# Four small groups of products per batch, issued as two pairs

## The chip, the cores and the metric

The kernel runs on one core of a Trainium2 chip. A core has a matrix engine (TensorE, PE in the profile; its weight loads are shown as PEld), a vector engine (VectorE, DVE), an activation engine (ScalarE, ACT), a general engine (GpSimd, POOL) and a queue engine that issues transfers (SyncE, SP). The metric is the time of one execution on the device, in microseconds (us); the median of several runs counts.

## The reference

The kernel computes a Fourier mixing followed by a feed-forward block with the quick form of GELU. The input x has 8 batches of 3008 rows and 256 columns.

```
X = fft(x, axis=1); X = fft(X, axis=2); y = X.real      # (8, 3008, 256) -> (24064, 256)
h = y @ w_in                                            # 256 -> 2048
g = h * (1 / (1 + exp(-1.702 * h)))
out = g @ w_out                                         # 2048 -> 256
```

## The kernel before

The transform along the 3008 rows is split, 3008 = 47 × 64. A first stage makes transforms of length 47 and a second stage transforms of length 64. The transform along the 256 columns is folded into the weights w_in before the main loop starts.

The main loop has 384 steps: 8 batches, 3 blocks to a batch, 2 halves to a block, and 8 pairs of feed-forward columns (p) to a half. So one batch lasts 48 steps. The order of work is written by hand: every engine has its own queue and works it off in the order in which the program issues to it. A step t issues, in this order:

- `hidden(t)` (L478): eight products with the folded weights, of 256 or 225 columns, into two banks, `pa` and `pb`, and on ScalarE a copy `v` of `pa` (L482). A product in float32 stands as two records in the profile, so `pa` and `pb` have four each.
- `product(t - 3)` (L551): seven products of the second layer (14 records), into banks of their own, `po`.
- `activate(t - 1)` on ScalarE (L507), then `sums(t - 1)` on GpSimd (L519, L520) and `sums(t - 2)` on VectorE (L522, L523).
- `rows(t)` on VectorE: L492 reads `v` and `pb`, L495 (twice) reads `pb`, L502 reads `pa`. After L495 the bank of `pb` is free, after L502 that of `pa`.
- every eighth step `combine` on VectorE (L585, L568), and output transfers from SP (L610).
- the extras of this step, from a table that is filled by `at(step, function, ...)`. They prepare the next batch.

The extras of a batch that starts at step t0 are (three steps later in the first batch): eight folds `fold1` on GpSimd (L195 to L202), one every second step from t0 + 7 on, that add and subtract rows of the next batch's tile `xt` in place; four groups of first-stage products `mix1` (L226) at t0 + 10, 14, 18 and 22, each one step after the second of the two folds that it needs; then `spill` of the result to memory at t0 + 24 (L302), `fill` from there in another layout at t0 + 29 (L308), the load of a further batch at t0 + 33 (L178). The second stage `stage2` (L328) comes at t0 + 8, 16 and 24.

One `mix1` group has eight products of 47 rows by 64 columns of weights (16 records). They go to the four quarters of the array in turn, since each needs only a quarter of it. The first group of a batch has 11 products (22 records), as one of its products is replaced by four of 127 to 129 columns from a small tile `e`. A group writes two banks, `ps[0]` and `ps[1]`, and then ScalarE copies each of them back into `xt` (L229).

`pa`, `pb`, the two banks of `mix1`, those of `stage2` and some small ones all come from one pool of four banks:

```
psm = ctx.enter_context(tc.tile_pool(name="psm", bufs=4, space=PS))
def bank(name):
    return psm.tile([128, 512], F32, tag="mm", name=name)
```

A tile takes a bank as soon as its earlier user has been read for the last time. In the program before, the products of `hidden` that follow a group take the banks of the `hidden` just ahead of the group: `pa` waits for L495 of that step, `pb` for L502. The step after that takes the banks of the group, behind its copies L229.

Of the kernel before, what the change touches and what calls it, by code (L numbers as in the profile page):

```python
# [111 lines left out]
def kernel(ctx: ExitStack, tc, x, w_in, w_out, tab1, tab2, out):  # L112
# [605 lines left out]
    def at(t, fn, *args):  # L718
        extra.setdefault(t, []).append((fn, args))
# [19 lines left out]
    for b in range(B):  # L739
        t0 = b * NBLK * NF  # L740
        late = 0 if b else 3
        if b + 2 < B:
            at(t0 + 10, turn, b + 2)
        if b + 1 < B:
            for c in range(NCH):
                at(t0 + 7 + 2 * c + late, fold1, b + 1, c, nc.gpsimd)
                if c % 2:
                    at(t0 + 8 + 2 * c + late, mix1, b + 1, c // 2)
            at(t0 + 24 + late, spill, b + 1)
            at(t0 + 29 + late, fill, b + 1)  # L750
            if b + 2 < B:
                at(t0 + 33 + late, load_x, b + 2)
            at(t0 + 36 + late, rotate, b + 1)
        for blk in range(NBLK):
            nxt = (b, blk + 1) if blk + 1 < NBLK else (b + 1, 0)
            if nxt[0] < B:
                at(t0 + blk * NF + 8, stage2, *nxt)
                at(t0 + blk * NF + 12, nyquist, *nxt)
# [53 lines left out]
```

## Time and profile before

| | |
|---|---|
| median of 6 runs | 1921.02 us (1920.35 to 1922.67) |
| the profiled execution's own time | 1922.67 us |
| its span, from the first to the last instruction | 1920.9 us |
| granted TensorE clock, mean over the span | 0.999 |
| TensorE busy | 1906.7 us, 99% |
| VectorE, ScalarE, GpSimd busy | 1419.4 us (74%), 674.7 us (35%), 761.4 us (40%) |
| L226, first-stage products | 490 records in 28 groups |
| L229, copies of their results | 56, 0.589 us each in the median |

The profile's chain follows the work back from the last instruction, always to what released it, and gives the share of each engine and line in that chain. The timeline gives rows of merged instructions: start in us, length in us, engine, line, operation, output<-inputs, sizes and count; a bracket behind a row says how long the engine was idle ahead of it and what ended that. The ends of products are modelled, so their starts are the better measure.

### The profile page before, as it was taken

The numbers are of one execution on the slowest core, as the hardware profiler recorded it, in microseconds if no ns is written. First come the engines' busy times: TensorE is split into PE (matmuls) and PEld (weight loads), VectorE is DVE, ScalarE is ACT, GpSimd is POOL, SyncE is SP. The second block draws the span as 40 slices with busy tenths as digits, with TensorE's granted clock in tenths as the row PEclk, the third lists the DMA queues.
The fourth block names the chain that finished last, engine by engine and source line by source line (L and its number), as shares of the span: only waits on it lengthen the run. The fifth ranks groups of instructions, "written<-read, shape, count | busy, mean of one in ns | idle before, by whom it ended". The sixth has DMA issues, their size and how long they took to land.

```text
span 1920.9 us, 29354 instructions
## 1 busy us (share of the span) xinstructions
PE 1906.7 (99%) x10720; PEld 1673.4 (87%) x10720; DVE 1419.4 (74%) x2937; ACT 674.7 (35%) x932; POOL 761.4 (40%) x1057
## 2 busy tenths in 40 slices
PE   8999999999999999999999999999999999999998
PEld 5798888988889888988889888898888988889887
DVE  7777677877787677777777777677777777778766
ACT  6533333333333333333333333333333333333332
POOL 4475224633246223552235523264323642223222
PEclk9999999999999999999999999999999999999999
DMA  8721530335212542226222272121820223202201
GB/s 267 177 50 34 114 37 12 59 53 106 17 22 49 91 67 23 52 27 103 44 28 50 43 105 34 16 49 43 124 19 12 17 49 56 17 12 27 17 12 23
DMA packets 145312, 103.54 MB, mean 54 GB/s; under 512 B 104914, under 2 KB 127986, under 8 KB 143984
## 3 DMA queue, kind: packets, MB, share of 16 engines
q1 hardware_dynamic: 143952, 101.14, 31.4%
q8 instruction: 85, 1.39, 0.3%
q10 hardware_dynamic: 1216, 0.52, 0.1%
q14 instruction: 59, 0.48, 0.1%
HBM read 58.38 MB, written 48.01 MB: 55 GB/s over the span
## 4 chain that ended last, share of the span: by engine, by line
PE 98%; DMA 1%; DVE 1%; POOL 0%; issue 0%; SPq 0%; ACT 0%; ACTq 0%; POOLq 0%
PE po L551 59%; PE pa L478 18%; PE pb L478 17%; PE ps L226 2%; PE ps L328 1%; DMA raw<-in_moe_w_in_dram 1%; PE psw L444 1%; DMA wo<-in_tab_dram 0%; POOL wst L420 0%; DVE m L406 0%; PE psf L454 0%; POOL m L379 0%; DVE a L408 0%; DVE a L407 0%; ACT h L507 0%
## 5 line engine op out<-in xcount | busy, mean ns | idle before, releaser
L551 PE MATMUL po<-s,wo 128*128 128x256 f32 (+1 forms) x3008 | 758.3, 375 | 0.0
L519 POOL TENSOR_TENSOR s<-h 128x256 f32<-128x256 f32 (+1 forms) x376 | 270.0, 718 | 1087.2 <-ACT h L507 1022.7
L551 PE MATMUL po<-h,wo 128*128 128x256 f32 (+1 forms) x2384 | 689.3, 375 | 0.0
L551 PEld LDWEIGHTS po<-s,wo 128*128 128x128 f32 x3008 | 571.5, 190 | 64.5
L482 ACT COPY v<-pa 128x512 f32<-128x512 f32 (+1 forms) x384 | 221.8, 578 | 1062.6 <-PE pa L478 1062.6
L492 DVE TENSOR_TENSOR h<-v,pb 128x512 f32<-128x512 f32 (+1 forms) x384 | 259.0, 674 | 396.1 <-PE pb L478 382.7
L551 PEld LDWEIGHTS po<-h,wo 128*128 128x128 f32 x2384 | 452.8, 190 | 51.6
L507 ACT ACTIVATE h<-h 128x1024 f32<-128x1024 f32 (+1 forms) x384 | 400.9, 1044 | 17.9 <-DVE h L502 15.5
L478 PE MATMUL pa<-pq,wcs 128*128 128x256 f32 (+1 forms) x1536 | 393.9, 379 | 1.9 <-ACT h L507 1.7
L478 PE MATMUL pb<-pq,wcs 128*128 128x256 f32 (+1 forms) x1536 | 387.5, 375 | 0.0
L478 PEld LDWEIGHTS pa<-pq,wcs 128*128 128x128 f32 x1536 | 286.7, 190 | 50.5 <-issue 10.4
L495 DVE SCALAR_TENSOR_TENSOR dif<-nb,af,pb 128x256 f32<-128x256 f32 (+1 forms) x768 | 328.4, 469 | 0.9 <-ACT nb L346 0.9
L478 PEld LDWEIGHTS pb<-pq,wcs 128*128 128x128 f32 x1536 | 291.7, 190 | 33.2
L520 POOL TENSOR_TENSOR s<-h 128x256 f32<-128x256 f32 (+1 forms) x376 | 275.7, 733 | 0.0
L502 DVE TENSOR_TENSOR h<-pa,dif 128x512 f32<-128x512 f32 (+1 forms) x448 | 265.5, 605 | 13.2
L523 DVE TENSOR_TENSOR s<-h,s 128x256 f32<-128x256 f32 (+1 forms) x376 | 202.3, 538 | 12.9
L522 DVE TENSOR_TENSOR s<-s,h 128x256 f32<-128x256 f32 (+1 forms) x376 | 179.7, 478 | 4.3 <-POOL s L519 4.3
L199 POOL TENSOR_TENSOR xt<-xt 111x510 f32<-111x510 f32 x56 | 73.1, 1305 | 4.4
L585 DVE TENSOR_TENSOR c<-u,po 128x256 f32<-128x256 f32 (+1 forms) x188 | 69.5, 410 | 2.5 <-PE po L551 0.9
L334 DVE STREAM_TRANSPOSE pq<-ps 128x256 f32<-128x256 f32 x96 | 34.6, 418 | 44.9 <-PE ps L328 44.9
L585 DVE TENSOR_TENSOR u<-u,po 128x256 f32<-128x256 f32 (+1 forms) x141 | 57.9, 410 | 8.2 <-ACT u L556 2.5
L568 DVE STREAM_TRANSPOSE os<-c 128x512 f32<-128x512 f32 x93 | 60.4, 687 | 0.0
(73 smaller groups left out, 509.3 us busy)
## 6 DMA issues: line engine op xcount, KB each, us to landing
out_dram<-os SPq DMA_DIRECT2D x284, 64.0 KB
Td<-xt SPq DMA_DIRECT2D x14, 768.0 KB
t<-Td SPq DMA_DIRECT2D x7, 1536.0 KB
xt<-in_x_dram SPq DMA_DIRECT2D x14, 512.0 KB
xt<-Xr SPq DMA_DIRECT2D x14, 512.0 KB
nb<-pq SPq DMA_DIRECT2D x23, 256.0 KB
out_dram<-os SPq DMA_DIRECT2D x96, 56.0 KB
Xr<-in_x_dram SPq DMA_DIRECT2D x7, 752.0 KB
```

Of the source, the lines that this page charges most:

```text
L478: nc.tensor.matmul(ps[:, i * 256:i * 256 + n], lhsT=wcs[cs][:, f * 128:(f + 1) * 128], rhs=pq[:, cs, ks], start=True, stop=True)
L482: nc.scalar.copy(two(v[:], n), two(pa[:], n))
L492: nc.vector.tensor_tensor(two(h[:], n), two(v[:], n), two(pb[:], n), op=ALU.add)
L495: nc.vector.scalar_tensor_tensor(dif[:, i * 256:i * 256 + n], nb[:, ks], af2[:, f:f + 1], pb[:, i * 256:i * 256 + n], op0=ALU.mult, op1=AL ...
L502: nc.vector.tensor_tensor(free(h[:], 512 + at + m - 1, [256, 2], [RUN, blocks], [-1, m]), *ins, op=ALU.add)
L507: nc.scalar.activation(g, g, ACTF.Gelu_apprx_sigmoid)
L519: eng.tensor_tensor(s1, a21, a22, op=ALU.add)
L520: eng.tensor_tensor(s3, a11, a21, op=ALU.subtract)
L522: eng.tensor_tensor(s2, s1, a11, op=ALU.subtract)
L523: eng.tensor_tensor(s4, a12, s2, op=ALU.subtract)
L551: nc.tensor.matmul(pot[q][:, i, :n], lhsT=lhs, rhs=rhs, start=(p == 0 and i == 0 and f == 0), stop=(p == NP - 1), skip_group_check=True)
L585: nc.vector.tensor_tensor(out_, i0, i1, op=how)
```

## The change

The four groups of a batch keep their products, their inputs and their copies. The first is issued in the same step as the second, directly ahead of it, and the third directly ahead of the fourth. So the first and third groups come four steps later than before, and the second and fourth stay where they were. At the two places a batch, both groups' products stand behind each other in TensorE's queue, and the four copies stand behind each other in ScalarE's.

```diff
         if b + 1 < B:
             for c in range(NCH):
                 at(t0 + 7 + 2 * c + late, fold1, b + 1, c, nc.gpsimd)
-                if c % 2:
-                    at(t0 + 8 + 2 * c + late, mix1, b + 1, c // 2)
+                if c % 4 == 3:
+                    for m in (c // 2 - 1, c // 2):
+                        at(t0 + 8 + 2 * c + late, mix1, b + 1, m)
             at(t0 + 24 + late, spill, b + 1)
             at(t0 + 29 + late, fill, b + 1)
```

A pair takes all four banks of the pool: its first group those of step t − 1, its second group those of `hidden(t)`. The `hidden` behind the pair then takes the two banks of the pair's first group: `pa` waits for the first copy L229, `pb` for the second. The `hidden` after that takes the banks of the second group. GpSimd and SP issue the same instructions in the same order as before.

## Prediction

> **What bounds the kernel now.** I read the busy shares first, then the chain of work that ended last, then TensorE's timeline at one group, then the engines that free and drain its banks.
>
> ```profile
> PE 1906.7 (99%) x10720; PEld 1673.4 (87%) x10720; DVE 1419.4 (74%) x2937; ACT 674.7 (35%) x932; POOL 761.4 (40%) x1057
> ...
> PE 98%; DMA 1%; DVE 1%; POOL 0%; issue 0%; SPq 0%; ACT 0%; ACTq 0%; POOLq 0%
> PE po L551 59%; PE pa L478 18%; PE pb L478 17%; PE ps L226 2%; PE ps L328 1%; DMA raw<-in_moe_w_in_dram 1%; PE psw L444 1%; DMA wo<-in_tab_dram 0%; POOL wst L420 0%; DVE m L406 0%; PE psf L454 0%; POOL m L379 0%; DVE a L408 0%; DVE a L407 0%; ACT h L507 0%
> ```
>
> TensorE is the bound, 98% of the chain (its granted clock over the span is 0.999). So a change is worth what it adds to or takes from TensorE's sequence, and L226, the first-stage products, holds only some 2% of it. This is that sequence around a fourth group (columns: start, length, engine, line):
>
> ```profile
> 616.24 1.03 PE L478 MATMUL pa<-pq,wcs 128*128 128x256 f32 x4
> ...
> 620.99 1.03 PE L478 MATMUL pa<-pq,wcs 128*128 128x256 f32 x4
> ...
> 625.31 0.59 PE L551 MATMUL po<-h,wo 128*128 128x256 f32 x2
> 625.83 1.09 PE L226 MATMUL ps<-xt,w 47*64 47x256 f32 x16
> 626.86 1.13 PE L478 MATMUL pa<-pq,wcs 128*128 128x256 f32 x4
> ...
> 631.71 1.03 PE L478 MATMUL pa<-pq,wcs 128*128 128x256 f32 x4
> ```
>
> A step without a group takes 620.99 − 616.24 = 4.75 us, the one with it 5.87, and the one behind it 4.85. The group costs 1.12 + 0.10 = 1.22 us. How much of that is streaming shows in a first group (568.69 on), whose records are not merged into one row:
>
> ```profile
> 569.18 0.38 PE L226 MATMUL ps<-xt,w 47*64 47x256 f32 x1
> ...
> 569.40 0.38 PE L226 MATMUL ps<-xt,w 47*64 47x256 f32 x1
> ...
> 569.62 0.59 PE L226 MATMUL ps<-xt,w 47*64 47x256 f32 x2
> 570.14 1.03 PE L478 MATMUL pa<-pq,wcs 128*128 128x225 f32 x4
> ```
>
> Products of 256 columns start 0.22 us apart in a quarter of the array. Sixteen records in four quarters are four rounds: 4 × 0.216 = 0.86 us (0.216 is 4.75 over the step's 22 records). The other 1.22 − 0.86 = 0.36 us is the passage from full-array to quarter products and back: some 0.09 going in (the last po pair runs 0.52 to the group where two records take 0.43), the rest coming out.
>
> **The change, part by part.** Counts of products, bytes and copies stay; SP and POOL issue the same things in the same order.
>
> *Passages removed.* Seven batches' groups make 28 passages before, 14 after. Joining a third group to a fourth saves one passage, 0.36 us. Joining a first to a second saves 0.02 less: the first group's 22 records are uneven, one quarter ends after the others, and the second group begins in just that quarter; its four rounds then add 0.86 and the 0.02 by which its quarters start after one another, 0.88 in place of 1.22, 0.34 saved. So 7 × 0.36 + 7 × 0.34 = 4.9 us less TensorE time, all on the chain.
>
> *Bound from both sides.* No row shows two groups end to end. At one end the passage stays inside the pair and the gain is 0. At the other, the second group also fills the three quarters that the first group leaves idle for its last round: 7 × 0.216 = 1.5 more, 6.4. I take 4.9, because rounds inside a group already follow without a gap.
>
> *Banks for the second of a pair.* The four rotating banks are all taken: the pair's first group takes those of step t − 1, the second those of hidden(t), freed by rows(t) on VectorE. The rows before the same place:
>
> ```profile
> 624.49 0.69 DVE L502 TENSOR_TENSOR h<-pa,dif 128x512 f32<-128x512 f32 x1
> ...
> 628.96 0.69 DVE L492 TENSOR_TENSOR h<-v,pb 128x512 f32<-128x512 f32 x1 [2.98 <-PE pb L478]
> ...
> 627.01 1.07 ACT L229 COPY xt<-ps 128x512 f32<-128x512 f32 x2 [3.36 <-PE ps L226]
> 628.08 0.58 ACT L482 COPY v<-pa 128x512 f32<-128x512 f32 x1
> ```
>
> L502 of that step ends at 625.18, 0.65 us before the pair would start and 1.5 before its second group. At 587.05, a second group, it ends at 586.64, 0.41 before. Cost 0; were DVE 1.5 us later, the wait would appear.
>
> *A new wait: the next pa behind the copies.* hidden(t+1) now takes the first group's banks, so pa waits for ScalarE's first L229 copy, pb for the second. With P the pair's start: copies start at P + 1.18 (627.01 − 625.83), the first ends at P + 1.77 (0.59 each), and pa is due at P + 1.03 + 0.86 = P + 1.89. A hand-off from ScalarE to TensorE is in the start-up: the copy of af ends at 47.41 + 0.16 = 47.57, pa's weights load at 47.62, 0.05. Margin 0.07 us. In the first-and-second pair the copy ends at P + 2.19 (570.29 − 568.69 + 0.59), pa is due at P + 1.45 + 0.88 = 2.33: 0.09. pb has over 0.4. I take 0. At the other end pa waits for both copies: P + 2.30 against 1.89 and P + 2.72 against 2.33, 0.4 × 14 = 5.6 us, the whole gain. Queued behind a waiting pa are all of hidden(t+1) and product(t−2).
>
> *Two more copies in ScalarE's row.* They end at P + 1.18 + 2.15 = 3.33, then v to P + 3.91; pb ends at 628.85, shifted to P + 3.88, and L492 started 0.11 behind it. In the first-and-second pair v comes 0.2 us late. The cover is VectorE's idle 2.98 us ahead of L492; its next deadline, the pb after, is a step (over 4 us) on. activate(t) is about 1.1 to 1.6 us later, so POOL's sums and VectorE's behind them; product(t), three steps on, is due over 6 us after its end (P + 5.3 at the latest, against P + 12). Cost 0; without that cover the two copies, 1.07 us a pair, would be 15.0.
>
> *Moved earlier work.* First and third groups go four steps later, past folds they don't need; POOL's L202 ended before every group. SP's spill waits for the pair's last copy, 1.1 us later than now; behind it are output stores and the fill. The fill is issued at 655.86, 27.7 us after the spill (628.15). Cost 0.
>
> **A rule against the row.** The trace puts 0.36 us on a passage. The Trainium skill, "TensorE: Matmul & The Clock Gate", section "Step-by-step: what each phase is for", says the drain is about 128 cycles at 2.4 GHz and overlaps the next fill between back-to-back matmuls; an estimate of one unhidden drain, 0.053 us, in and out, would make the gain 14 × 0.107 = 1.5 us and the time 1919.5. Against the change speaks "TensorEngine Tiling (Array Packing)", section "PSUM Bottleneck": packing speeds up TensorE but not the emptying of PSUM, which may then bound it, and it advises using VectorE beside ScalarE; here four copies stand in ScalarE's row alone, and by that rule the last rival below would be the likeliest. The trace has ScalarE 35% busy and idle 3.36 us ahead of the copies, so I go by the rows.
>
> **Sum.** −4.9 us. The profiled execution took 1922.67 us, with a span of 1920.9 and 1.8 around it: 1917.8 for it. It is 1.65 above the median of the six runs, 1921.02, from which I forecast 1916.1, or 0.25% faster. A measurement can tell about 0.2%, 3.8 us, here: 1917.2 is the bound.
>
> **Rivals.**
> - *pa waits for the copies.* For: a margin of 0.07 to 0.09 us. Against: the same hand-off takes 0.05, and at 117.16 pa started without idle after a VectorE release (L495, 116.14 + 0.80) some 0.2 us ahead. Midway, 0.2 us a pair: 2.8 back, 1918.9. Within 0.2%.
> - *The passage stays inside the pair*, because the second group's bank waits stop its weights being loaded ahead. For: no row shows the joint. Against: those semaphores are up over 1 us early, and single groups also carry waits in the middle. 1921.0. Within 0.2%.
> - *Slower: ScalarE's row of four copies.* Place: v(t+1) and activate(t), then POOL, then VectorE, whose in-order queue keeps rows(t+2) behind sums(t). Price: 1.07 us a pair, 15.0 − 4.9 = +10.1, 1931.1. It decides once activate(t) is late by more than VectorE's wait for pb, some 1.2 to 3 us; I work out 1.1 to 1.6. Against: the lag of three steps.
>
> **How the numbers follow.** Forecast 0.68, its own range 1914.6 (the gain of 6.4) to 1917.2; pa's wait 0.16; passage kept 0.08; ScalarE slower 0.08. Faster takes 0.68 and 0.02 of pa's smallest waits: 0.70. Same 0.22, slower 0.08. The range 1914.5 to 1919.6 holds the forecast and most of pa's waits; kept passage, slower case and the tail of pa's waits, 0.2 in all, lie outside.
>
> **What the profile after would show.** L226 in 14 places instead of 28, each with 32 or 38 records; a fourth-group pair running from P to pa at P + 1.89; the pa record behind it without idle released by ACT xt L229; four L229 copies in a row of about 2.15 us; DVE's L492 still released by PE pb. Wrong if pa starts later than P + 1.95, if a gap over 0.1 us stands between the pair's halves, or if PEld idles on L229, POOL or DVE by more than 0.1 us a pair.

## The result

The changed kernel takes 1916.48 us (median of 18 runs, 1915.28 to 1917.92), the kernel before 1921.75 us (38 runs, 1920.01 to 1922.99). The ratio is 0.9973, with a 95% interval from 0.9967 to 0.9980: 0.27% faster, or 5.2 us (3.8 to 6.3). The forecast was 1916.1 us.

The page of the profiled execution after, with the lines that answer to those shown of before:

```profile
PE 1900.8 (99%) x10720; PEld 1676.2 (88%) x10720; DVE 1412.2 (74%) x2937; ACT 675.0 (35%) x932; POOL 765.9 (40%) x1057
...
PE 98%; DMA 1%; DVE 1%; POOL 0%; issue 0%; SPq 0%; ACT 0%; ACTq 0%; POOLq 0%
PE po L551 60%; PE pa L478 17%; PE pb L478 17%; PE ps L226 2%; PE ps L328 1%; DMA raw<-in_moe_w_in_dram 1%; PE psw L444 1%; DMA wo<-in_tab_dram 0%; POOL wst L420 0%; DVE m L406 0%; PE psf L454 0%; POOL m L379 0%; DVE a L408 0%; DVE a L407 0%; ACT h L507 0%
```

TensorE is still the bound, with the same 10720 records; it is busy 5.9 us less. The span went from 1920.9 to 1915.4 us, 5.5 us. Not all of that is the change, as the next view shows: one line of the answer on L478, first of the kernel before, then of the changed one (count, shortest, median and longest record in ns, first and last start in us).

```profile
L478 PE MATMUL pa<-pq,wcs x1536: 353/379/483, 41.5 to 1901.3; 128*128 128x256 f32 x160, 128*128 128x225 f32 x32
```

```profile
L478 PE MATMUL pa<-pq,wcs x1536: 353/379/483, 41.1 to 1895.9; 128*128 128x256 f32 x160, 128*128 128x225 f32 x32
```

From the first to the last `pa` record, before and after: 1901.3 − 41.5 = 1859.8 us, and 1895.9 − 41.1 = 1854.8 us. The main loop is 5.0 us shorter; the other 0.4 us lie ahead of it. The start-up differs from execution to execution (in the runs below the first `pa` starts between 38.5 and 41.1 us), so I compare this stretch, "the loop" from here on, beside the timed medians.

TensorE's timeline after, at the pair that holds a fourth group, in the same batch as the rows shown before:

```profile
617.59 1.03 PE L478 MATMUL pa<-pq,wcs 128*128 128x256 f32 x4
...
621.91 0.59 PE L551 MATMUL po<-h,wo 128*128 128x256 f32 x2
622.43 1.96 PE L226 MATMUL ps<-xt,w 47*64 47x256 f32 x32
624.32 1.13 PE L478 MATMUL pa<-pq,wcs 128*128 128x256 f32 x4
...
629.17 1.03 PE L478 MATMUL pa<-pq,wcs 128*128 128x256 f32 x4
```

(`hidden` has four products, two for each bank, so `pa` and `pb` have four records each, and a plain step has these 8 and the 14 of `product`.) The 32 records of two groups run as one stretch; `pa` follows 624.32 − 622.43 = 1.89 us after the pair's start, where one group took 1.03. The step with the pair takes 6.73 us and the one behind it 4.85, so with 4.75 for a plain step the pair costs 1.98 + 0.10 = 2.08 us, against 2 × 1.22 = 2.44 for two single groups: 0.36 us saved.

ScalarE and VectorE at the same place:

```profile
623.56 2.05 ACT L229 COPY xt<-ps 128x512 f32<-128x512 f32 x4 [3.31 <-PE ps L226]
625.54 0.58 ACT L482 COPY v<-pa 128x512 f32<-128x512 f32 x1
```

```profile
621.09 0.69 DVE L502 TENSOR_TENSOR h<-pa,dif 128x512 f32<-128x512 f32 x1
...
626.42 0.69 DVE L492 TENSOR_TENSOR h<-v,pb 128x512 f32<-128x512 f32 x1 [3.85 <-PE pb L478]
```

The four copies take 2.05 us in a row from 1.13 us after the pair's start, `v` follows, and L492 is still released by `pb`, with 3.85 us of idle VectorE ahead of it. The longer row on ScalarE delays nobody on the path: from 100 to 1900 us TensorE's own list of waits is empty, before as after.

One line of the list of waits can mislead here. After the change it names ScalarE's copy ahead of `pa`'s weight loads, which it never did before:

```profile
PEld pa L478 <- ACT xt L229: 5.4, 14, 0.4
PEld pa L478 <- issue: 4.6, 23, 0.2
```

Fourteen times 0.39 us, once for each pair, look like the new wait that the first rival feared. They are not. Before, the weight loads behind each of the 28 groups had the same 0.39 us, put down 14 times to "issue" and 14 times to VectorE. One row of before and one of after, each at the fourth group shown:

```profile
626.85 0.73 PEld L478 LDWEIGHTS pa<-pq,wcs 128*128 128x128 f32 x4 [0.39 <-issue]
```

```profile
624.32 0.73 PEld L478 LDWEIGHTS pa<-pq,wcs 128*128 128x128 f32 x4 [0.39 <-ACT xt L229]
```

I read it as the time in which the weight loader stands still while the array goes back to the full shape, put down to whoever released last. That `pa` did not wait shows in its start: it comes 0.31 us after the last record of the group in both kernels (28 and 14 times in the trace).

### The profile page after: what moved, and what is told of

Read it like the earlier page. It is cut to its first block, busy times and chain, and to the rows that moved or that the text cites. A ratio compares the mean times of both kernels' runs of the same rounds, so it can differ in the third digit from the quotient of the medians.

```text
span 1915.4 us, 29378 instructions
## 1 busy us (share of the span) xinstructions
PE 1900.8 (99%) x10720; PEld 1676.2 (88%) x10720; DVE 1412.2 (74%) x2937; ACT 675.0 (35%) x932; POOL 765.9 (40%) x1057
## 4 chain that ended last, share of the span: by engine, by line
PE 98%; DMA 1%; DVE 1%; POOL 0%; issue 0%; SPq 0%; ACT 0%; ACTq 0%; POOLq 0%
PE po L551 60%; PE pa L478 17%; PE pb L478 17%; PE ps L226 2%; PE ps L328 1%; DMA raw<-in_moe_w_in_dram 1%; PE psw L444 1%; DMA wo<-in_tab_dram 0%; POOL wst L420 0%; DVE m L406 0%; PE psf L454 0%; POOL m L379 0%; DVE a L408 0%; DVE a L407 0%; ACT h L507 0%
## 5 line engine op out<-in xcount | busy, mean ns | idle before, releaser
L492 DVE TENSOR_TENSOR h<-v,pb 128x512 f32<-128x512 f32 (+1 forms) x384 | 258.8, 674 | 398.2 <-PE pb L478 387.5
L478 PE MATMUL pa<-pq,wcs 128*128 128x256 f32 (+1 forms) x1536 | 392.4, 378 | 1.9 <-ACT h L507 1.7
L478 PE MATMUL pb<-pq,wcs 128*128 128x256 f32 (+1 forms) x1536 | 387.6, 375 | 0.0
L478 PEld LDWEIGHTS pa<-pq,wcs 128*128 128x128 f32 x1536 | 287.8, 190 | 45.5 <-ACT xt L229 5.4
L478 PEld LDWEIGHTS pb<-pq,wcs 128*128 128x128 f32 x1536 | 291.8, 190 | 33.1
L502 DVE TENSOR_TENSOR h<-pa,dif 128x512 f32<-128x512 f32 (+1 forms) x448 | 265.5, 605 | 13.2
L522 DVE TENSOR_TENSOR s<-s,h 128x256 f32<-128x256 f32 (+1 forms) x376 | 172.2, 458 | 4.3 <-POOL s L519 4.3
```

Of the source, the lines that this page charges most:

```text
L478: nc.tensor.matmul(ps[:, i * 256:i * 256 + n], lhsT=wcs[cs][:, f * 128:(f + 1) * 128], rhs=pq[:, cs, ks], start=True, stop=True)
L492: nc.vector.tensor_tensor(two(h[:], n), two(v[:], n), two(pb[:], n), op=ALU.add)
L502: nc.vector.tensor_tensor(free(h[:], 512 + at + m - 1, [256, 2], [RUN, blocks], [-1, m]), *ins, op=ALU.add)
L522: eng.tensor_tensor(s2, s1, a11, op=ALU.subtract)
```

## Experiments

The theory: a visit of TensorE to quarter products (the prediction's "passage", there and back) costs 0.36 us, whatever the number of products in it, and the change removes 14 of 28 visits. The rivals: the gain comes from the new places of the first and third groups or from their banks; or the cost of a visit sits in the length of a group. Two further questions: how near the copies on ScalarE came to costing something, and what a still longer visit would give.

| kernel | visits by the first stage | median, us | ratio to before (95%) | loop, us | loop less before |
|---|---|---|---|---|---|
| before | 28 | | | 1859.8 | |
| changed | 14 | 1916.48 | 0.9973 (0.9967 to 0.9980) | 1854.8 | −5.0 |
| pair pulled apart | 28 | 1921.45 | 1.0003 (0.9994 to 1.0012) | 1859.8 | 0.0 |
| groups in halves | 56 | 1932.47 | 1.0060 (1.0047 to 1.0074) | 1871.1 | +11.3 |
| pairs, one copy more | 14 | 1919.83 | 0.9999 (0.9990 to 1.0007) | 1858.7 | −1.1 |
| all four in one go | 7 | 1917.92 | 0.9985 (0.9977 to 0.9994) | 1856.8 | −3.0 |
| the same, copies on two engines | 7 | 1914.72 | 0.9969 (0.9958 to 0.9981) | 1853.8 | −6.0 |
| the same, joined to the second stage | 7 | 1913.13 | 0.9962 (0.9949 to 0.9976) | 1852.5 | −7.3 |
| pairs, copies on two engines | 14 | 1915.61, one run | | 1854.8 | −5.0 |

The kernel before, run on the same chips beside these kernels, had a median of 1920.36 us beside the first four experiments and 1921.22 us beside the last three. So the ratios can be compared, the medians less well. Each loop is that of one profiled execution, with a granted clock of 0.999 or 1.000.

### The pair pulled apart in its own step

```diff
                 if c % 4 == 3:
-                    for m in (c // 2 - 1, c // 2):
-                        at(t0 + 8 + 2 * c + late, mix1, b + 1, m)
+                    mid[t0 + 8 + 2 * c + late] = mix1, (b + 1, c // 2 - 1)
+                    at(t0 + 8 + 2 * c + late, mix1, b + 1, c // 2)
...
         if t == 0:
             ...
+        if t in mid:
+            fn, args = mid[t]
+            fn(*args)
...
         if t >= LAG:
             product(t - LAG)
```

> The pair is pulled apart inside its step: its first group is issued between the step's pa/pb products and the step's po products, its second group behind the po products as now. Steps, banks and copies stay, only the contact of the two groups is undone, so there are 28 passages again. Passage theory (0.36 us for each passage from full-array to quarter products and back): 14 x 0.36 = 5.0 us more than the changed kernel, about 1921.5 us, the time of before; each visit shows about 0.09 us of delay going in, pa or po 0.31 us behind the last group record and 0.10 us between the next two records. Place theory (the gain came from where the first and third groups stand now, or from their banks and waits): the time stays at 1916.5 us.

TensorE's timeline of this run:

```profile
617.91 1.03 PE L478 MATMUL pb<-pq,wcs 128*128 128x256 f32 x4
618.87 1.09 PE L226 MATMUL ps<-xt,w 47*64 47x256 f32 x16
619.89 0.70 PE L551 MATMUL po<-h,wo 128*128 128x256 f32 x2
...
622.59 0.59 PE L551 MATMUL po<-h,wo 128*128 128x256 f32 x2
623.11 1.09 PE L226 MATMUL ps<-xt,w 47*64 47x256 f32 x16
624.14 1.13 PE L478 MATMUL pa<-pq,wcs 128*128 128x256 f32 x4
```

Both groups stand in the step of the pair, in the pair's banks; the products `po` are between them, and in ScalarE's row the first group's copies now come 4.25 us before the second's (620.05 and 624.30). Each costs 1.02 to 1.03 us to the next record again, the loop has the length of before to the tenth, and the time is that of before (1.0003). The whole gain hangs on the contact of the two groups on TensorE. Place and banks are out as its source.

### Every group in two halves

```diff
-                if c % 2:
-                    at(t0 + 8 + 2 * c + late, mix1, b + 1, c // 2)
+                if c % 2:
+                    mid[t0 + 8 + 2 * c + late] = mix1, (b + 1, c // 2, 0)
+                    at(t0 + 8 + 2 * c + late, mix1, b + 1, c // 2, 1)
...
-    def mix1(b, m):
+    def mix1(b, m, half):
-        ps = [bank("ps1") for _ in range(2)]
+        if half == 0:
+            open_ps[b, m] = [bank("ps1") for _ in range(2)]
+        ps = open_ps[b, m]
-        for i in (2 * m, 2 * m + 1):
+        for i in (2 * m + half,):
...
+        if half == 0:
+            return
         for r in range(2):
             nc.scalar.copy(...)
```

> The kernel before, with each of the 28 groups cut into two halves of four products, one half ahead of the step's po products and one behind them, both into the same two banks, copies at the end as before: 56 passages with the same products. Passage theory: 28 x 0.36 = 10.1 us more than before, about 1931.8 us. If a good part of the 0.36 us belonged to the length of a group (its uneven first round, waits that stand in it) and not to the passage, the cost of the 28 new passages would be nearer to 0.2 us each, about 1927 us.

Two halves of one group in this run's timeline (L230 is `mix1` here, L557 `po`, L484 `pa` and `pb`):

```profile
626.61 1.03 PE L484 MATMUL pb<-pq,wcs 128*128 128x256 f32 x4
627.57 0.66 PE L230 MATMUL ps<-xt,w 47*64 47x256 f32 x8
628.16 0.70 PE L557 MATMUL po<-h,wo 128*128 128x256 f32 x2
...
631.38 0.66 PE L230 MATMUL ps<-xt,w 47*64 47x256 f32 x8
631.97 1.13 PE L484 MATMUL pa<-pq,wcs 128*128 128x256 f32 x4
```

A half of 8 records takes 0.59 us to the next record, where 16 take 1.03 and 32 take 1.89. The steps between them are 0.44 for 8 records more and 0.86 for 16 more, so 0.43 us for 8 records and a rest that doesn't depend on the length: 0.59 − 0.43 = 0.16, to which come 0.10 going in and 0.10 behind. That is 0.36 us a visit once more. 28 visits more are 10.1 us. The loop is 11.3 us longer; the other 1.2 us stand in one place, the first half of the first batch's first group, 0.70 us of idle ahead of it and 0.52 us within it. It now stands ahead of the `po` products, in a step in which VectorE is late, and starts just after VectorE's release of its first bank (112.46 + 0.79 = 113.25). Its second bank is free when L508 of that run (L502 before) ends at 113.98, and the weights for it load at 114.05:

```profile
113.29 0.69 DVE L508 TENSOR_TENSOR h<-pa,dif 128x448 f32<-128x448 f32 x2
113.33 0.19 PEld L230 LDWEIGHTS ps<-e,w 47*64 47x64 f32 x2 [0.95 <-issue]
113.36 0.29 PE L230 MATMUL ps<-e,w 47*64 47x129 f32 x1 [0.63 <-issue]
...
114.05 0.17 PEld L230 LDWEIGHTS ps<-xt,w 47*64 47x64 f32 x2 [0.41 <-issue]
```

### How near the copies came: one copy more ahead of the pair's four

```diff
+        if m % 2 == 0:
+            nc.scalar.copy(xt[:, 4 * m, :], ps[0][:, 0:D])
         for r in range(2):
             nc.scalar.copy(free(xt[:], (4 * m + r) * D, [2 * D, 2], [1, D]), free(ps[r][:], 0, [D, 2], [1, D]))
```

> The changed kernel with one more ScalarE copy ahead of the pair's four (the first half of the same bank to the same place, so the result stays): the first L229 copy ends about 0.32 us later, and with it the release of the bank that pa waits for. In the changed kernel the first copy ends 1.72 us after the pair's start, pa starts at 1.89, the hand-off takes 0.05: margin 0.12 us. Margin theory: pa starts 0.20 us late, 14 x 0.20 = 2.8 us more than the changed kernel, about 1919.3 us, with TensorE idle that is released by the copy L229. Rival (this wait is not near the path, there is slack somewhere that I don't see): no change, 1916.5 us.

ScalarE and TensorE in this run (L231 are the four copies, L480 is `pa`):

```profile
623.23 0.37 ACT L229 COPY xt<-ps 128x256 f32<-128x256 f32 x1 [3.31 <-PE ps L226]
623.63 2.05 ACT L231 COPY xt<-ps 128x512 f32<-128x512 f32 x4
```

```profile
622.10 1.96 PE L226 MATMUL ps<-xt,w 47*64 47x256 f32 x32
624.27 1.13 PE L480 MATMUL pa<-pq,wcs 128*128 128x256 f32 x4 [0.21 <-ACT xt L231]
```

The first real copy starts 1.53 us after the pair's start in place of 1.13, 0.40 late, and `pa` starts at 2.17 in place of 1.89, 0.28 late. The margin is the difference, 0.12 us, as reckoned; the added copy was 0.08 us longer in effect than I had taken it (0.40, not 0.32). Fourteen times 0.28 is 3.9 us, which is what the loop shows (1858.7 − 1854.8), and nearly the whole gain is gone. Here TensorE itself, not only its weight loader, has an idle row with L231 as its releaser: that is what a real wait for the copies looks like, beside the harmless line above.

### All four groups in one go

```diff
-                if c % 4 == 3:
-                    for m in (c // 2 - 1, c // 2):
+                if c == 7:
+                    for m in range(4):
                         at(t0 + 8 + 2 * c + late, mix1, b + 1, m)
```

> All four groups of a batch behind one another in the step of the fourth: 7 passages. Passage theory alone: 7 x 0.36 = 2.5 us less than the changed kernel, 1914.0 us. But the third group now takes the banks of the first: ScalarE ends the first group's second copy some 2.65 us after the start, the third group wants that bank at 2.23 us, a wait of about 0.45 us; the fourth waits some 0.15 us more for the second group's copies. 7 x 0.6 = 4.2 us of waits, so I expect about 1918.2 us: slower than the pairs, faster than single groups. If ScalarE's copies were of no account, 1914.0 us.

```profile
618.09 0.32 PE L226 MATMUL ps<-e,w 47*64 47x129 f32 x1
...
622.76 1.13 PE L478 MATMUL pa<-pq,wcs 128*128 128x256 f32 x4
```

`pa` comes 4.67 us after the start. By the pairs it would be 2.31 us for a first and a second group and 0.86 for each further one, 4.04 in all. So 0.63 us a batch are waits for banks, 4.4 us in all, more than the 2.5 us that seven visits are worth. ScalarE's copies at this place:

```profile
619.64 4.01 ACT L229 COPY xt<-ps 128x512 f32<-128x512 f32 x8 [3.73 <-PE ps L226]
```

They start 1.55 us after the first product and take about 0.5 us each, two to a group, where a group takes 0.86 us; four banks hide that for two groups and not for more. The fourth copy frees the second bank of the fourth group. By the trace it ends 3.61 us after the start, and the products that need this bank start at 3.66, where they were due at 1.36 + 2 × 0.86 = 3.08 (1.36 is a first group's 1.45 to `pa`, less the 0.31 of the way out, with 0.22 for its last round). The other 0.05 us are their first round, which takes 0.27 us and not 0.22 as at the start of a visit. The loop is 2.0 us longer than that of the changed kernel; 1.7 were expected.

### The same with the second copy of each group on VectorE

```diff
-            nc.scalar.copy(free(xt[:], (4 * m + r) * D, ...
+            (nc.vector.tensor_copy if r else nc.scalar.copy)(free(xt[:], (4 * m + r) * D, ...
```

> All four groups in one go as in the earlier run, but of each group's two copies the second goes to VectorE, so that two engines empty the banks. Waits: the third group wants the first one's banks 2.22 us after the start; ScalarE frees one at 2.19, VectorE (0.69 us for such a read) the other at about 2.29, so about 0.07 us is left of the 0.61 us that the copies cost on ScalarE alone. Passage theory: 21 passages fewer than before, 21 x 0.36 = 7.5 us, less 7 x 0.1 of waits: 6.8 us faster than before, 1.8 us faster than the pairs. If the waits of the earlier run were not for the copies but for something that four groups in a row do to TensorE, it stays at 3 us faster than before.

```profile
617.03 0.32 PE L226 MATMUL ps<-e,w 47*64 47x129 f32 x1
...
621.28 1.13 PE L478 MATMUL pa<-pq,wcs 128*128 128x256 f32 x4
```

4.25 us from start to `pa`: of the 0.63 us a batch, 0.21 are left, so the waits were for the copies. The loop is 6.0 us shorter than before, where I had expected 6.8: I had reckoned with the banks of the third group only. What is left stands ahead of the fourth:

```profile
619.47 0.58 ACT L229 COPY xt<-ps 128x512 f32<-128x512 f32 x1 [0.29 <-PE ps L226]
619.52 0.69 DVE L229 COPY xt<-ps 128x512 f32<-128x512 f32 x1 [0.65 <-PE ps L226]
620.10 0.79 PEld L226 LDWEIGHTS ps<-xt,w 47*64 47x64 f32 x16 [0.26 <-ACT xt L229]
```

The fourth group's products are due at 617.03 + 1.36 + 2 × 0.86 = 620.11. ScalarE's copy ends at 620.05, and by the trace the products into its bank start at 620.11, on time. VectorE's copy takes 0.69 us, ends at 620.22, and the products into its bank start at 620.27, 0.16 us late; their first round again takes 0.05 us more than the later ones. That makes the 0.2 us, in all seven batches alike. So what is left hangs on the slower copy on VectorE, as read from the starts; no run changed that copy alone.

### Joined to the second stage

```diff
-                        at(t0 + 8 + 2 * c + late, mix1, b + 1, m)
+                        at(t0 + (25 if late else 24), mix1, b + 1, m)
```

> The same, with the four groups issued in the step of the third second-stage block and directly ahead of its products (in six of seven batches; in the first batch one step behind it, as that step comes before the last fold). Second-stage products use the array in eighths, first-stage products in quarters. If leaving the quarters for the eighths costs a passage like leaving them for the full array, the time is that of the four groups alone, 6.8 us faster than before. If only the way from and to the full array costs, one passage a batch goes: 6 x 0.36 = 2.2 us more, 9 us faster than before, less some 0.1 us a batch where the second stage waits for the third group's banks. The boundary itself shows in the start times: 0.31 us from the last first-stage record to the first second-stage record if it costs, 0.2 if it does not.

```profile
631.55 0.60 PE L226 MATMUL ps<-xt,w 47*64 47x256 f32 x6
632.08 1.16 PE L328 MATMUL ps<-t,small 64*32 64x128 f32 x64
633.17 1.13 PE L478 MATMUL pa<-pq,wcs 128*128 128x256 f32 x4
```

(The second stage comes at t0 + 8, 24 and 40; the groups now stand directly ahead of the one at t0 + 24, in six of the seven batches.) The last first-stage record starts at 631.55 + 0.60 − 0.38 = 631.77, and the second stage 0.31 us later: leaving the quarters costs the same whether eighths or the full array come next. Saved is only the second stage's own way in and the slow first weights behind one of the two visits, 0.10 + 0.10 us. Six joints make 1.2 us; the loop is 1853.8 − 1852.5 = 1.3 us shorter. The boundary shows the 0.31 us of the first expectation, yet the gain lies between the two. It is the fastest version of this study (0.9962, 0.9949 to 0.9976), though its interval overlaps those of the one above and of the changed kernel.

### Pairs with copies on two engines

The changed kernel, with the second copy of each group on VectorE as above.

> The changed kernel, pairs, with the second copy of each group on VectorE. pa waits for the first copy, which stays on ScalarE at the same time, and nothing else of the pair waits for a copy: pa at 1.89 us after a fourth-group pair's start as with ScalarE alone, the main loop as long as in the changed kernel within 0.3 us. If the copies bound the pair, it would be shorter by 14 times what they cost.

```profile
620.79 1.96 PE L226 MATMUL ps<-xt,w 47*64 47x256 f32 x32
622.67 1.13 PE L478 MATMUL pa<-pq,wcs 128*128 128x256 f32 x4
```

1.88 us, and a loop of 1854.8 us, that of the changed kernel. In this one execution a second engine on the copies brings nothing: for pairs the copies cost nothing.

## Why the prediction was right, point by point

- *TensorE's sequence is all that counts.* Right: the chain is 98% TensorE before and after, and every experiment's time follows from TensorE's rows.
- *Fewer passages, 0.36 us each.* Right, and shown three ways: the pair's rows, the pair pulled apart (0.0), and the halves (0.36 for each of 28 added visits, with the 1.2 us of one bank wait taken off).
- *0.02 us less for a first with a second group.* Not so. In the timeline after, the first group of such a pair starts at 583.59 and `pa` at 585.90: 2.31 us, not 2.33. All 14 joints saved 0.36 us, so the sum is 14 × 0.36 = 5.0 us and not 4.9. The prediction let the second group begin in the quarter that ends late. It begins in the three idle ones:

```profile
584.52 1.46 PE L226 MATMUL ps<-xt,w 47*64 47x256 f32 x18
585.90 1.03 PE L478 MATMUL pa<-pq,wcs 128*128 128x225 f32 x4
```

The row of 18 holds the last two records of the first group and all 16 of the second. By the trace three of the second start at 584.52 to 584.53, the first group's last at 584.73. So the filling of idle quarters, which the larger end of the bound put at 1.5 us, did come, and it saved nothing: the quarter that ends late still has four rounds of the second group to do, 4 × 0.216 = 0.86 us, and `pa` follows 0.31 us behind the start of the last of them.

- *Banks of the second group.* Right: L502 ended at 621.78, 0.65 us before the pair.
- *The new wait of `pa` for the first copy.* Right that it costs 0; the margin was 0.12 us and not 0.07, as the copies started 1.13 us and not 1.18 us after the pair's start. One copy ahead of them was enough to cost 3.9 us, so this rival was a near one. For the one delay that was tried, 0.40 us, what went beyond 0.12 us was lost, 14 times.
- *Two more copies on ScalarE.* Right: they took 2.05 us (2.15 reckoned), and L492 stayed with `pb` as its releaser. The slower rival needed activate and VectorE to be late beyond a step's slack; VectorE had 3.85 us of idle time at that place.
- *The rules.* The estimate from the Trainium skill's page "TensorE: Matmul & The Clock Gate" (Step-by-step: what each phase is for) was a gain of 1.5 us; the measured 5.0 us is over three times that, so one drain of the array each way does not describe a passage here. The Trainium skill's page "TensorEngine Tiling (Array Packing)" (PSUM Bottleneck) warns that the emptying of PSUM, here the banks, may come to bound a packed array: for pairs it did not, for four groups in a row it did. There the copies on ScalarE cost 4.4 us, and the page's advice to use VectorE as well brought back 3.0 us of it (1856.8 − 1853.8).
- *The signs.* L226 stands in 14 places with 32 or 38 records, `pa` starts at P + 1.89, and the pair's halves run as one row. One sign of being wrong did show: the weight loader idles on L229 by 0.39 us a pair, over the 0.1 us named. It was a bad sign, since the same 0.39 us stand behind all 28 groups before.
- *The number.* That 1916.1 came within 0.4 us of 1916.48 is partly luck. It started from a median of 1921.02 us, 0.7 below the 1921.75 that the kernel before took beside the changed one, and its gain of 4.9 was 0.4 below the 5.3 between the two medians; the errors partly cancel. The 5.0 us of the loop are the better test of the sum.

## What to carry to other kernels

On an engine that never idles, look for work that changes the shape in which the array is used, and cost the change of shape apart from the products: take the time from neighbour to neighbour and subtract the products at the pace that they keep among themselves. Here a visit cost 0.36 us beside 0.86 us of work, and putting two visits together was worth all of that. How many could be put together was set by the banks and by who empties them, and since the margin was 0.12 us, it had to be worked out to a tenth of a microsecond before.

## What the runs showed that I had not expected

- Leaving the quarter shape costs 0.31 us from the last record's start also when the next products use the array in eighths; only the way in from the full array (0.10 us) and the slow first weights behind a visit (0.10 us) are saved by such a neighbour.
- A bank freed by ScalarE 0.06 us ahead of its products cost nothing in the middle of a stretch; the last 0.2 us of wait in the stretch of four groups hung on the other copy, 0.69 us on VectorE.
- A second group that begins in idle quarters 0.2 us early gains nothing when one quarter ends late and has as many rounds left as the others.
- An idle row of the weight loader changes its releaser with the program while its length stays (0.39 us behind each visit): the name in the list of waits told nothing about a wait there, and the start of the next product did.
